# Placing the attention steps of batches 2 to 5 anew, with V moved on hardware queues and loads tied to slots

## The chip, the cores and the metric

The kernel runs on one core of a Trainium2 chip. The metric is the device time of one execution in microseconds (us), lower is better. Eight executions of the kernel before gave a median of 354.93 us, from 352.25 to 355.64. The profile shows one of these executions (352.25 us) in full; its span from the first to the last instruction is 350.5 us.

The engines are TensorE (PE in the profile; PEld is its weight load), VectorE (DVE), ScalarE (ACT), GpSimd (POOL) and SyncE (SP). DMAs are issued by POOL (a software queue, q0), or by SP and ACT (hardware queues, q1). Every engine runs its own instructions in the order of the program and waits on semaphores of the others.

## What is computed

Two stages, in float32 at the outside:

```python
batch, n_heads, seq, head_dim = (8, 8, 576, 64)
n_tokens, d_model, d_ff = (4608, 512, 2048)

def _attn_ref(q, k, v):                      # window = 64, causal
    scores = scale * np.matmul(q, k.transpose(0, 1, 3, 2))
    mask = (rel >= 0) & (rel < window)       # rel = query position - key position
    attn = softmax(np.where(mask, scores, -1e9))
    return np.matmul(attn, v)

def _moe_ref(x, w_in, w_out):
    h = x @ w_in
    return (h - np.tanh(h)) @ w_out
```

The attention's output, heads side by side, is x with 4608 rows of 512. The kernel computes in bf16 with float32 sums.

## The kernel before

**Units.** A batch b is one of 8 sequences of 576 tokens with 8 heads. A group g = 4b + pr is a pair of heads of a batch, 32 groups in all. A window j is 64 queries, 9 to a batch, each with 128 keys. A chunk c is 512 tokens of x, 9 in all; chunk 2 needs x of batches 1 and 2, chunk 3 of batches 2 and 3, chunk 4 of 3 and 4, chunk 5 of 4 and 5.

**The two-layer part.** `hp_mm(c, m)` is four matmuls of 512 columns for one of 16 slices m of the hidden layer (L393), then `Tanh` on ACT (L398); `g_sub(c, m)` subtracts on DVE and leaves gT (L405). `yp_mm` is four of the matmuls of the output (L417); every fourth one is followed by `y_out`, a copy on ACT (L422) and a DMA to the output on SP (L424). A hidden slice has a bank of PSUM: m % 3 in chunks 0 to 2, m % 2 after; the bank is free when `g_sub` has read it.

**Slots.** The order of all this is written out by hand as numbered slots. `OPS` gives each slot at most one piece of the two-layer part: slots 0 to 31 the hidden layer of chunk 0 (every second one), 32 to 47 the output of chunk 0, 48 to 63 hidden 1, 64 to 79 output 1, 80 to 95 hidden 2, and from 96 on hidden c and output c - 1 in turn, 32 slots to a chunk. `at(h, fn, ...)` hangs a step of the attention on slot h. The loop at the end of the kernel goes through the slots and emits, for each, first the two-layer piece, then its steps in the order of their `at` calls, then `g_sub`:

```python
for fn, args in items.pop(h, []):
    fn(*args)
if op and op[0] == "h":
    g_sub(*op[1:])
```

A slot is a place in the order and not a time: an engine that has nothing to wait for runs ahead of the others' slots.

**The steps of a group** from batch 2 on are: `cast` of q and of k (rows reordered into qb and kb, on DVE or POOL, L86), `tr` of q and of k (six transposes each on PE, L267, in bank 3; the q result goes out half on ACT and half on DVE, L84 and L86, the k result on ACT), `scores` three times (three matmuls each, L334, in bank 4, then `Exp` on ACT, L336), `masking` (DVE, L340), and the product with V. That product is `tile_pv` in batches 0 to 3 (20 matmuls of 65 columns, L322, banks 6 and 7, then one reciprocal and one multiplication on DVE, L326 and L328) and `pv` three times with `norm` in batches 4 to 7 (nine matmuls of 130 columns, L346, banks 5 to 7, then one reciprocal and two multiplications of 64 partitions, L353 and L357). The result xs is turned by `x_tr` (transposes on PE, L363, copied out on DVE or ACT) in batches 0 to 3 and by `x_dma` (two DMA transposes on SP, L378) in batches 4 to 7.

**V.** `load_v_all` brings V of a batch from DRAM (one buffer, vall), `cast_v` reorders it, four calls to a batch, into vb (one buffer as well), and nine `keys_v` or `windows_v` are DMAs from vb into vw, one per window (L161, L176; two buffers of vw, by the batch's parity). `pv` of windows 3i to 3i + 2 waits for these three.

**Loads** of q and k are issued on POOL, either per group (`load`, 144 KB as written) or per batch (`load_all`, 576 KB). `pace(h)` is a copy of one element on POOL that waits for the last `g_sub` before slot h, so that a load behind it doesn't start earlier.

Around the change the order before is this. Batch 0's nine `keys_v` and batch 1's are all on POOL. In slots 48 and 49 POOL has `cast_v(2)` four times, nine `windows_v(2)`, `load_v_all(3)`, and in slot 50 the eight loads of groups 12 to 15; in slots 55 and 56 it has the casts of group 10. Batch 3 is placed at slots 62 to 95, batch 4 from 69 on, batch 5 from 86 on.

## Time and profile before

| what | value |
|---|---|
| median of 8 executions (lowest, highest) | 354.93 us (352.25, 355.64) |
| profiled execution: its time, its span | 352.25 us, 350.5 us |
| granted TensorE clock, mean | 0.969 |
| PE, PEld busy | 318.8 us (91%), 173.3 us (49%) |
| DVE, ACT, POOL busy | 201.1, 184.9, 113.5 us (57, 53, 32%) |
| chain that ended last: PE, DMA, POOL, DVE, ACT | 67, 14, 7, 4, 3% of the span |
| start of slot 32, 48, 64, 80 | 41.44, 67.64, 92.69, 115.80 us |
| start of slot 96, 128, 160 | 143.03, 180.27, 214.07 us |

How to read it. The start of a slot is the start of its first L393 or L417 matmul in the timeline. Matmuls of 512 columns follow each other every 0.216 us, so four of them take 0.86 us in the chain of waits, although the page lists a mean of 385 ns for one; PE that counts as busy may still be waiting between two of them. A line of the timeline has the start, the time from the first start to the last end of a run of like instructions, the engine, the line of the kernel, the tiles and, in brackets, the idle time before it and what ended that.

### The profile page before, as it was taken

The page shows a single profiled execution, that of the slowest core. Times are in us where ns is not written, and L with a number is a line of the kernel's source. Part 1 is how long each engine was busy: PE and PEld are TensorE (multiplying, and loading weights), DVE is VectorE, ACT ScalarE, POOL GpSimd, SP SyncE. Part 2 cuts the span into 40 slices and gives each one's busy share as a digit, 9 for nine tenths or more (in the row PEclk, how much of TensorE's full clock was granted, in tenths as well). Part 3 has the DMA queues.
Part 4 walks back from the last instruction along what each step waited for, and adds up shares of the span by engine and source line. Part 5 has one row for each costly group of instructions (what it writes and reads, how often), then busy time and mean ns, then how long its engine had stood idle before and what let it go on. Part 6 is the DMA issues. An engine that isn't in the chain of part 4 may idle for free.

```text
span 350.5 us, 6289 instructions
## 1 busy us (share of the span) xinstructions
PE 318.8 (91%) x2452; PEld 173.3 (49%) x2452; DVE 201.1 (57%) x336; ACT 184.9 (53%) x336; POOL 113.5 (32%) x169
## 2 busy tenths in 40 slices
PE   6769989794999868899899999999999999999994
PEld 2544444452555544555555555555555444444442
DVE  4565766883665667577666767766666444444300
ACT  3534534584555767466566666655554444444411
POOL 8860166684713613362362553610000000000000
PEclk9568999999899999999999999999999999999999
DMA  8999999989399169528499598689921400100021
GB/s 156 149 178 215 194 166 154 174 138 165 45 154 236 51 98 163 76 61 139 100 160 166 107 170 145 126 163 211 191 63 51 109 30 30 55 36 30 32 90 61
DMA packets 51398, 42.39 MB, mean 121 GB/s; under 512 B 21176, under 2 KB 44664, under 8 KB 51368
## 3 DMA queue, kind: packets, MB, share of 16 engines
q0 software_dynamic: 21728, 20.40, 38.8%
q1 hardware_dynamic: 29432, 21.30, 26.0%
q8 instruction: 19, 0.31, 0.4%
q10 hardware_dynamic: 208, 0.29, 0.3%
q14 instruction: 11, 0.09, 0.1%
HBM read 36.70 MB, written 11.21 MB: 137 GB/s over the span
## 4 chain that ended last, share of the span: by engine, by line
PE 67%; DMA 14%; POOL 7%; DVE 4%; ACT 3%; issue 3%; POOLq 0%; ACTq 0%; DVEq 0%; SPq 0%
PE ps L417 30%; PE ps L393 27%; DMA vall<-in_v_dram 10%; PE ps L334 3%; PE ps L267 3%; PE ps L346 2%; POOL vw L176 2%; DMA qall<-in_q_dram 2%; DMA kall<-in_k_dram 1%; PE ps L322 1%; POOL vb L86 1%; POOL vw L161 1%; DVE gT L405 1%; DMA kt<-kd 1%; ACT pt L336 1%
## 5 line engine op out<-in xcount | busy, mean ns | idle before, releaser
L393 PE MATMUL ps<-xT,wi 128*128 128x512 bf16 x576 | 146.7, 385 | 3.1 <-DVE gT L405 2.4
L405 DVE TENSOR_TENSOR gT<-ps,th 128x512 bf16<-128x512 f32 x144 | 98.8, 690 | 84.1 <-ACT th L398 82.3
L417 PE MATMUL ps<-w_out_sb,gT 128*128 128x512 bf16 x576 | 143.9, 379 | 0.0
L398 ACT ACTIVATE th<-ps 128x512 f32<-128x512 f32 x144 | 85.6, 597 | 76.4 <-PE ps L393 74.9
L393 PEld LDWEIGHTS <-wi 128*128 128x128 bf16 x576 | 61.9, 114 | 52.0 <-issue 6.9
L417 PEld LDWEIGHTS <-gT 128*128 128x128 bf16 x576 | 53.3, 98 | 53.8 <-issue 0.2
L336 ACT ACTIVATE pt<-ps 128x384 bf16<-128x384 f32 x72 | 35.2, 489 | 31.7 <-PE ps L334 31.4
L86 POOL COPY vb<-vall 72x1024 bf16<-72x1024 bf16 x24 | 24.8, 1052 | 32.4 <-DMA vall<-in_v_dram 20.1
L422 ACT ACTIVATE ysb<-ps 128x512 f32<-128x512 f32 x36 | 21.6, 599 | 18.6 <-PE ps L417 18.6
L86 DVE COPY qt<-ps 64x576 bf16<-64x576 bf16 x20 | 15.2, 760 | 21.6 <-ACT qt L84 21.6
L334 PE MATMUL ps<-qt,kt 128*128 128x128 bf16 x216 | 23.9, 220 | 2.1 <-ACT pt L336 1.4
L357 DVE TENSOR_TENSOR xs<-ps,rc 64x576 bf16<-64x576 f32 x32 | 24.2, 755 | 0.8
L334 PEld LDWEIGHTS <-kt 128*128 128x128 bf16 x216 | 16.1, 98 | 12.3 <-issue 2.2
L340 DVE TENSOR_TENSOR pt<-pt,ps 128x1152 bf16<-128x1152 bf16 x24 | 17.9, 744 | 1.1 <-ACT pt L336 1.1
L346 PEld LDWEIGHTS <-pt 128*128 128x128 bf16 x144 | 12.0, 98 | 12.5 <-issue 1.3
L346 PE MATMUL ps<-vw,pt 128*128 128x130 bf16 x144 | 16.0, 220 | 1.0 <-DVE xs L357 1.0
L86 POOL COPY qb<-qall 96x768 bf16<-96x768 bf16 x15 | 12.4, 825 | 11.5 <-DMA qall<-in_q_dram 7.7
L86 POOL COPY kb<-kall 96x768 bf16<-96x768 bf16 x19 | 15.7, 832 | 0.0
L84 ACT ACTIVATE qt<-ps 64x576 bf16<-64x576 bf16 x20 | 12.7, 635 | 5.6 <-PE ps L267 5.6
L97 POOL DMA_DIRECT2D qall<-in_q_dram x15 | 9.7, 647 | 18.1 <-DMA vall<-in_v_dram 10.5
L267 PE MATMUL ps<-ident,qb 96*128 96x96 bf16 x120 | 8.6, 209 | 6.0 <-POOL qb L86 4.9
L84 ACT ACTIVATE kt<-ps 128x576 bf16<-128x576 bf16 x20 | 13.0, 648 | 1.4 <-PE ps L267 1.4
(74 smaller groups left out, 212.1 us busy)
## 6 DMA issues: line engine op xcount, KB each, us to landing
out_dram<-ysb SPq DMA_DIRECT2D x36, 256.0 KB, 2.1
vw<-vb SPq DMA_DIRECT2D x40, 130.0 KB, 4.2
vall<-in_v_dram POOLq DMA_DIRECT2D x7, 576.0 KB, 11.2
kall<-in_k_dram POOLq DMA_DIRECT2D x4, 576.0 KB, 9.5
qall<-in_q_dram POOLq DMA_DIRECT2D x4, 576.0 KB, 9.0
kall<-in_k_dram POOLq DMA_DIRECT2D x15, 144.0 KB, 10.2
qall<-in_q_dram POOLq DMA_DIRECT2D x15, 144.0 KB, 9.9
wi<-in_moe_w_in_dram POOLq DMA_DIRECT2D x2, 1024.0 KB, 11.3
```

What stands on the lines that cost most here:

```text
L84: nc.scalar.activation(o, i, ACT.Copy)
L86: eng.tensor_copy(o, i)
L267: nc.tensor.transpose(tp[:, e, :], src[:, e, :], ident[:P, :P])
L334: nc.tensor.matmul(sp[:, i, :], kT[g % NR][:, 64 * j:64 * j + 128], qT[g % NR][:, :, 64 * j:64 * j + 64], start=True, stop=True)
L336: nc.scalar.activation(PT[g % NPT][:, 3 * grp:3 * grp + 3, :], sp, ACT.Exp, scale=scale)
L346: nc.tensor.matmul(ps[:, 5 + grp, 130 * i:130 * i + 130], PT[g % NPT][:, j, :], vw[b % 2][:, j, 2 * pr:2 * pr + 2, :], start=True, stop=True)
L357: nc.vector.tensor_tensor(xo[r, :, :, pr, :], ov[r, :, :, h, 0:D], rc[r].to_broadcast([64, 3, 3, 64]), ALU.mult)
L393: nc.tensor.matmul(hp, w_in_tile(ki, m), chunk_tile(c)[:, :, ki % 2, 64 * (ki // 2):64 * (ki // 2) + 64], start=(ki == 0), stop=(ki == 3))
L398: nc.scalar.activation(th, hp, ACT.Tanh)
L405: nc.vector.tensor_tensor(gT[c][:, m, :], hp, th, ALU.subtract)
L417: nc.tensor.matmul(yp, gT[c][:, m, s * 128:(s + 1) * 128], w_out_sb[:, m, :], start=(m == 0), stop=(m == M - 1))
L422: nc.scalar.activation(ysb, ps[:, yp_bank(c, s), :], ACT.Copy)
```

## The change

Four things are done; the computation is the same.

1. `keys_v` of batch 0: windows 0 and 3 on SP, 1 and 4 on ACT, the other five on POOL. `keys_v` of batch 1: by turns on POOL and SP.
2. Batch 2: `cast_v` moves from POOL in slot 48 to DVE in slot 46; `windows_v` from POOL in slot 49 to SP in slot 47. Batch 3's loads become three loads of a whole batch at slots 54 (k, behind a `pace`), 55 (q) and 56 (v), in place of v at 49 and eight loads at 50. Its `cast_v` moves from slots 62 to 65 to 67 to 70, its `windows_v` from 67 to 71.
3. Groups 8 to 15 take their slots from a table, with `pv` and `norm` (all in one slot, `whole_pv`) in place of `tile_pv`. `x_tr` of batch 2 goes to bank 0, and batch 3 uses `x_dma` in slot 92 in place of four `x_tr`.
4. Batches 4 and 5 get other slots for groups, `cast_v`, `windows_v` and loads (batch 4's loads at 77, 78, 79 in place of 71, 72, 69; batch 5's at 97, 98, 99 in place of 86, 89, 92), the loads of batch 5 wait for `x_dma(3)` as well (`behind_x`), and `load_all` of batch 6 goes from slots 124 and 128 to 128 and 130. From slot 148 on the placing is as before.

```diff
--- before.py
+++ after.py
@@ -481,8 +481,8 @@
     copy_mask()
     tile_scores(0, 0, (0, 1))
     tile_scores(0, 1, (4, 5))
-    for j in range(NJ):
-        keys_v(0, j, G)
+    for j, eng in enumerate((Y, A, G, Y, A, G, G, G, G)):
+        keys_v(0, j, eng)
     load_w_in(0)
     load_w_in(1)
     load_w_out(0)
@@ -524,7 +524,7 @@
 
     at(33, lambda: [cast_v(1, pr, V) for pr in range(NP)])
     at(34, more_constants)
-    at(35, lambda: [keys_v(1, j, G) for j in range(NJ)])
+    at(35, lambda: [keys_v(1, j, (G, Y)[j % 2]) for j in range(NJ)])
     at(35, load, 7, "q", G)
     at(35, load_v_all, 2)
     for g in 8, 9, 10, 11:
@@ -561,68 +561,77 @@
     at(47, x_tr, 1, 1, 0, 4, 3, V)
     at(47, x_tr, 1, 1, 4, 9, 6, A)
 
+    at(46, lambda: [cast_v(2, pr, V) for pr in range(NP)])
+    at(47, lambda: [windows_v(2, j, Y) for j in range(NJ)])
+    at(54, pace, 54)
+    at(54, load_all, 3, "k")
+    at(55, load_all, 3, "q")
+    at(56, load_v_all, 3)
     for pr in range(NP):
-        at(48, cast_v, 2, pr, G)
-    at(49, lambda: [windows_v(2, j, G) for j in range(NJ)])
-    at(49, load_v_all, 3)
-    for g in range(12, 16):
-        at(50, load, g, "k", G)
-        at(50, load, g, "q", G)
+        at(67 + pr, cast_v, 3, pr, G)
+    at(71, lambda: [windows_v(3, j, Y) for j in range(NJ)])
     for i in range(2):
         at(140 + 4 * i, more_zeros, i)
 
-    def std(g, ck, cq, t, tk, ss, ms, p):
-        at(cq, cast, g, "q", V if g not in (10, 11, 15) else G)
-        at(ck, cast, g, "k", V if g not in (10, 11, 15) else G)
-        at(t, tr, g, "q", 3, A, V)
+    def whole_pv(g):
+        for i in range(3):
+            pv(g, i)
+        norm(g)
+
+    STEPS = {
+        8: (48, V, 50, 52, (55, 57, 59), 61, 63),
+        9: (52, V, 55, 57, (60, 61, 62), 64, 66),
+        10: (55, G, 60, 62, (64, 65, 66), 68, 70),
+        11: (59, G, 64, 65, (68, 69, 70), 71, 74),
+        12: (64, V, 67, 68, (72, 73, 74), 76, 78),
+        13: (68, V, 71, 72, (76, 77, 78), 80, 83),
+        14: (71, G, 75, 76, (80, 82, 84), 86, 88),
+        15: (75, G, 79, 81, (85, 86, 87), 88, 91),
+    }
+    for g, (c, eng, tq, tk, ss, ms, p) in STEPS.items():
+        at(c, cast, g, "q", eng)
+        at(c + 1, cast, g, "k", eng)
+        at(tq, tr, g, "q", 3, A, V)
         at(tk, tr, g, "k", 3, A)
         for i in range(3):
-            at(ss + 2 * i, scores, g, i, 4)
+            at(ss[i], scores, g, i, 4)
         at(ms, masking, g)
-        at(p, tile_pv, g, (6, 7))
-
-    for i, g in enumerate(range(8, 12)):
-        a = (50, 55, 60, 65)[i]
-        lead = 3 if i < 2 else 5
-        std(g, a - lead + 1, a - lead, a, a + 2, a + 3, a + 8, a + (12 if i == 0 else 11))
-    at(70, x_tr, 2, 0, 0, 4, 3, V)
-    at(71, x_tr, 2, 0, 4, 9, 3, A)
-    at(78, x_tr, 2, 1, 0, 4, 3, V)
-    at(79, x_tr, 2, 1, 4, 9, 3, A)
-
-    for g in range(3 * NP, B * NP):
+        at(p, whole_pv, g)
+    at(71, x_tr, 2, 0, 0, 4, 0, V)
+    at(72, x_tr, 2, 0, 4, 9, 0, A)
+    at(77, x_tr, 2, 1, 0, 4, 0, V)
+    at(78, x_tr, 2, 1, 4, 9, 0, A)
+    at(92, x_dma, 3)
+
+    def behind_x(b):
+
+        last = ((b + 1) * NJ - 1)
+        nc.gpsimd.tensor_copy(tick, chunk_tile(last // WPC)[0:1, last % WPC, 0, 0:1])
+
+    LOADS = {4: (77, 78, 79), 5: (97, 98, 99), 6: (128, 130, 113)}
+    for g in range(4 * NP, B * NP):
         b, pr = divmod(g, NP)
-        a = 8 * g - 48 - (0, 2, 4)[min(b - 3, 2)]
-        s = 32 * b - (0, 2, 4)[min(b - 3, 2)]
+        a = 8 * g - 52
+        s = 32 * b - 4
         cv, ky = s - 72 + 5 * pr, s - 54
-        if b == 3:
-            a = (68, 73, 78, 82)[pr]
-            cv = 62 + pr
-        elif b == 4:
-            a = 84 + 7 * pr
-            cv, ky = 75 + 3 * pr, 86
+        if b == 4:
+            a = (89, 95, 101, 108)[pr]
+            cv, ky = 91 + pr, 95
         elif b == 5:
-            cv, ky = 95 + 4 * pr, 108
+            a = 110 + 7 * pr
+            cv, ky = 108 + pr, 112
+        elif b == 6:
+            cv = 118 + 4 * pr
         at(cv, cast_v, b, pr)
-        if b == 3:
-            lead = 3 if pr < 3 else 6
-            std(g, a - lead + 1, a - lead, a, a + 2, a + 3, a + 8, a + 11)
-            if pr == 0:
-                for j in range(NJ):
-                    at(67, windows_v, b, j, Y)
-            if pr % 2:
-                at(a + 12, x_tr, b, pr // 2, 0, 4, 3, V)
-                at(a + 13, x_tr, b, pr // 2, 4, 9, 3, A)
-            continue
         if b < 7:
-            at(a - 7, cast, g, "q")
+            at(a - (5 if b < 6 else 7), cast, g, "q")
             at(a, tr, g, "q", 3, A, V)
         else:
             at(a - 14, cast_q, g)
             at(a - 12, bounce, g, "q")
             at(a - 6, tr_dma, g, "q")
         if b < 7:
-            at(a - 5, cast, g, "k")
+            at(a - (4 if b < 6 else 5), cast, g, "k")
             at(a + 2, tr, g, "k", 3, A)
         else:
             at(a - 13, cast, g, "k")
@@ -638,16 +647,14 @@
             at(a + 16, x_dma, b)
         for j in range(NJ):
             if pr == 0:
-                at(ky + (j // 2 if b > 5 else 0), windows_v, b, j, Y)
+                at(ky + j // 2, windows_v, b, j, Y)
         if pr == 0:
-            if b > 3:
-                hq, hk = s - (60 if b < 7 else 68), s - (64 if b < 7 else 72)
-                hv = {4: 69, 5: 92}.get(b, s - 78)
-                if b < 6:
-                    hk, hq = {4: (71, 72), 5: (86, 89)}[b]
-                for h, f in (hv, (load_v_all, b)), (hq, (load_all, b, "q")), (hk, (load_all, b, "k")):
-                    at(h, pace, h)
-                    at(h, *f)
+            hk, hq, hv = LOADS.get(b, (s - 72, s - 68, s - 78))
+            for h, f in (hv, (load_v_all, b)), (hq, (load_all, b, "q")), (hk, (load_all, b, "k")):
+                at(h, pace, h)
+                if b == 5:
+                    at(h, behind_x, 3)
+                at(h, *f)
 
     for h in range(32 * NC + 32):
         op = OPS.get(h)
```

## The prediction

> **What bounds the kernel now.** I read the busy times by stage first, cut at the starts of slots 32, 48, 64, 80, 96 and 128. Columns: stretch, its length, busy time and (instructions) of PE, PEld, DVE, ACT, POOL, then clock, DMA share, GB/s.
>
> ```profile
> 41.44:67.64 26.20, 22.04 (x284) 12.00 (x283) 18.27 (x39) 11.53 (x20) 15.38 (x23) 1.00 1.09 178
> 67.64:92.69 25.05, 19.39 (x144) 10.67 (x142) 16.04 (x26) 15.19 (x30) 18.32 (x28) 0.93 0.79 122
> 92.69:115.80 23.11, 21.28 (x237) 12.04 (x234) 12.76 (x24) 12.08 (x26) 6.27 (x10) 1.00 0.87 160
> 115.80:143.03 27.23, 21.42 (x221) 12.64 (x216) 20.04 (x33) 20.05 (x40) 10.70 (x15) 1.00 0.65 104
> 143.03:180.27 37.24, 36.09 (x278) 20.87 (x278) 25.40 (x40) 22.91 (x44) 16.80 (x21) 1.00 0.57 99
> 180.27:350.50 170.23, 165.58 (x954) 86.33 (x952) 84.80 (x130) 82.94 (x146) 24.56 (x36) 1.00 0.47 100
> ```
>
> PE's own work I count from start-to-start distances in the timeline: 0.864 us for a two-layer piece (four at 0.216), 0.25 for a `tr`, 0.17 for `scores` or a third of `pv`, 0.54 for `tile_pv`, 0.055 for a transpose of x. That gives 20.84, 16.96, 20.30, 19.76 and 35.04 us for the first five stretches, so PE loses 5.36, 8.10, 2.81, 7.46 and 2.20 us in them, 25.9 in all, and only 0.9 in the last. The change lies in these five.
>
> The chain of waits from 60 to 100 us (start, length, what) shows the largest loss:
>
> ```profile
> 64.88 4.03 POOL vb L86 x4
> ...
> 74.16 11.23 DMA vall<-in_v_dram
> ...
> 86.29 0.85 POOL qb L86
> ...
> 87.19 0.66 PE ps L267 x6
> 87.85 2.83 PE ps L393 x8
> ```
>
> and the timeline says why:
>
> ```profile
> 80.32 0.63 POOL L97 DMA_DIRECT2D kall<-in_k_dram  x1
> ...
> 85.67 0.63 POOL L97 DMA_DIRECT2D qall<-in_q_dram  x1 [4.72 <-DMA vall<-in_v_dram]
> ...
> 87.19 0.66 PE L267 MATMUL ps<-ident,qb 96*128 96x96 bf16 x6 [4.85 <-POOL qb L86]
> ```
>
> POOL issues V of batch 3 and seven of eight loads, then stands still until V has landed; the cast of group 10 is queued behind, and PE waits 4.85 us. Each of POOL's stalls of this kind (four more from 25 to 42 us, one at 64.25) ends when the oldest of eight loads lands, so I read it as eight in flight at most. After the wait eight matmuls take 2.83 us in place of 1.73.
>
> Two other losses: slot 37's transposes wait for a cast that stands in DVE's queue behind V of batch 1 (landed 44.9), and hidden 2 loses 7.5 us in pieces of 0.5 to 1.3 to evacuations of bank 3 and to ACT and DVE, each 20 us busy of 27:
>
> ```profile
> 47.93 0.43 PE L287 MATMUL ps<-ident,kb 96*128 96x96 bf16 x6 [1.14 <-DVE kb L86]
> ...
> 128.97 0.41 PE L267 MATMUL ps<-ident,kb 96*128 96x96 bf16 x6 [1.06 <-ACT xT L84]
> ```
>
> [...] `windows_v` issued on SP lands in 3.8 us with no load near and in 7.2 to 9.4 beside one. [...] Here an issue of vall takes 0.85 us, its landing 7.4 to 13.5 beyond batch 1. [...] here `cast_v` is 1.05 us against 0.43.
>
> **The change, part by part**, in the profile's own time (350.5 span, 352.25 for that execution).
>
> *Start to slot 48.* POOL loses 4 of 9 `keys_v`, each about 0.58, and four places of the eight: the first w_in, issued at 16.08, goes at about 13, and all loads behind it land some 2.5 us earlier, V of batch 1 at 42.3. Two issues on ACT (0.4 to 0.7 each, between 11.15 and 12.5) push ACT's chain of batch 0 by 0.1 to 0.6; hidden 0 waits 0.49 for w_in now, so its start moves -0.5 to +0.6, I take -0.15. Slot 37's wait, 1.33 with its tail, goes: -1.5 so far. In batch 1 POOL issues 5 `keys_v` in place of 9, so V of batch 2 is issued at about 48.5 in place of 52.74 and lands (11.2 later at most) by 60, just before DVE wants it. But four `cast_v` on DVE, 4 x 0.43 = 1.72, now stand before batch 1's last products, where DVE has 0.2 to 0.4 us free and x of batch 1 is next: +1.5. With V late they would cost up to 2 us more. Hidden 1 starts at 67.6, as before.
>
> *Hidden 1.* POOL's 20.6 us (4 casts of V, 9 moves, 9 loads, 4 casts) shrink to 6.0, and three loads are far from eight: the cast of group 10 is done at about 79, its transposes come at 81. The wait and the cold clock go. Left are PE's work of 16.9 and DVE's sum of 17.6 (16 `g_sub` at 0.69, casts, two masks, one norm), which I price at 2 us of loss: 18.9 in place of 25.05. Slot 64 at 86.5, -6.2.
>
> *Output 1.* PE's work rises by 0.7 (batch 3's groups come earlier). The waits of bank 3 go, DVE's backlog (norm 0.21 + 2 x 0.755 = 1.72 in place of 1.04 for each of eight groups) costs about as much. Here V is the question. The load of k is tied to slot 54: issue 76.7; k, q, v together take some 15.5 (8 small loads and V took 14.1 from 77.2 to 91.3): V of batch 3 lands at 92.2. `cast_v` 4.2 to 96.4, nine moves on SP, 10 to 12 us to the last landing (11 in batch 5's case now): 108.5. Slot 78 has `pv(12)` and would come at 106 or 107. So slot 80 is at about 110.5, -5.3.
>
> *Hidden 2.* Two `tile_pv` and three x transposes fewer for PE (17.55 us of work), ACT falls from 20.5 to 15.6, DVE stays at 20.0 and leads: masks 13 to 15, norms 13 to 15, `g_sub` and one copy make 16.6 until norm 15, which ends 17.2 after slot 80, at 127.7. `x_dma(3)` lands 3.4 later (median of the first ones; 3.3 to 4.7 over all), where four x transposes, 1 us, and their evacuations stood. Slot 96 at about 131.4, -11.6.
>
> *Slots 96 to 127.* Loads of batch 5 wait for `x_dma(3)`: k issued at 134, V landed at 152, later than the 146.6 now. `cast_v` to 156.4, moves until 167 to 170, beside V of batch 6. On POOL `cast_v(6)` stands before the cast of group 22 and must wait until the moves have read vb; so `tr(22)` in slot 124 is ready at 170.4, against 165.9 for PE. `pv(20)` also stands directly behind `pv(19)` in slot 123 and waits for a norm, 1.9. In all 5.4 given back: slot 128 at 174.0 in place of 180.27, -6.2.
>
> *After.* `load_all(6)` is one to two slots nearer to its use; now q lands 1.5 us ahead of need. I take 0.6 (0 to 2). The rest, without loss now, stays.
>
> Sum: -1.5 + 1.5 - 6.2 + 0.9 - 6.3 + 5.4 + 0.6 = -5.6: 352.25 becomes 346.6. That execution was the fastest of eight, 2.7 below the median; on the median I predict 349.3.
>
> **Rivals.** A measurement of this kernel can tell 0.5% (1.8 us) from no change.
> 1. *The chain of V keeps up.* Loads and moves a few us faster than taken, and nothing is given back after slot 96: -11.6, 343.3. For it: moves with no load beside them land in 3.8. Against: V of batch 5 lands later than now by the sum above.
> 2. *V late from batch 3 on: slower.* From slot 78 on the path runs V landed, casts on POOL, moves on SP, norm, `x_dma(3)`, loads of batch 5, one us for one. If V of batch 3 lands at 97.8 in place of 92.2 all is gone; 1.8 later still it is slower. Batch 4's three loads now take 22.3 from first issue to last landing (94.72 to 117.02) beside nine moves; that puts V at 99, +1.2, and the same again in batch 5 about +3: 359. Against: no moves stand beside batch 3's loads in the new order.
> 3. *The stall stays under another name.* Group 10's casts are still on POOL, behind two or three large issues; if these block as the small ones did, the 4.85 us remain and with the extra DVE work the gain is near 0: 355. Against: batches 4 and 5 issue three such loads now without a stop over 1.04.
>
> **How the numbers follow.** Forecast 0.45, rival 1 0.23, rival 2 0.22, rival 3 0.10. The range reaches from rival 1 (342.5) to most of rival 2 (358); the forecast's own is 346 to 352.5. Faster by over 0.5%: the forecast but a few per cent, and rival 1, 0.64; within: 0.12; slower: 0.24.
>
> **What would show it.** No wait of `tr` for qb near slot 60 and hidden 1 near 19 us (rival 3 if not); slot 37 without a wait; four vb copies on DVE of 0.43 each without a wait before them; last moves of batch 3 landed at 108 to 109, and a wait of `pv(12)` of 1 to 3 us; slot 96 at 131 (over 136: rival 2); a wait of slot 124's transposes for qb of 3 to 5 us (none: rival 1). If hidden 1 saves less than 4 us, or DVE waits for V in slot 46, the forecast is wrong from there.

## The result, and the profile after

The changed kernel takes 359.25 us (median of 11 executions, 355.89 to 362.15), the kernel before 354.28 in the same session (32 executions). The ratio is 1.0129, with a 95% interval from 1.0100 to 1.0158: slower by 1.3%, where 349.3 us was predicted. The profiled execution took 359.56 us, its span 357.8 us. Here and below the ratios leave out executions more than 1.5% above the fastest of their kernel (9 of 22 of `a_win4`, 2 of 6 of `c_three`) and the medians don't, so a ratio can differ by up to 0.4% from what two medians give.

Each kernel has a second profile (`before_look` and `after_look`, single executions of 351.92 and 357.38 us, below), so there are two values. "Predicted" is in the profile's own time. "After against predicted" takes the first profile.

| start of | before | predicted | after | after against predicted |
|---|---|---|---|---|
| slot 48, hidden 1 | 67.64 / 71.26 | 67.6 | 67.81 / 67.77 | +0.2 |
| slot 64, output 1 | 92.69 / 92.28 | 86.5 | 88.97 / 87.58 | +2.5 |
| slot 80, hidden 2 | 115.80 / 115.37 | 110.5 | 116.04 / 114.51 | +5.5 |
| slot 96 | 143.03 / 142.59 | 131.4 | 139.71 / 138.17 | +8.3 |
| slot 128 | 180.27 / 179.83 | 174.0 | 186.97 / 184.92 | +13.0 |
| end of span | 350.5 / 350.2 | 344.9 | 357.8 / 355.7 | +12.9 |

The change leads by 3.7 us at slot 64, and by 3.3 at slot 96; between 96 and 128 it loses 10.0. The prediction misses 2.3, 3.0, 2.8 and 4.7 us in four stages in a row. The busy times by stage of the changed kernel, cut at the starts of slots 32, 48, 64, 80, 96 and 128 (stretch, length, busy time and instructions of PE, PEld, DVE, ACT, POOL, clock, DMA share, GB/s):

```profile
41.90:67.81 25.91, 22.36 (x283) 12.51 (x282) 18.97 (x43) 11.53 (x20) 9.78 (x16) 0.96 1.06 183
67.81:88.97 21.16, 20.39 (x129) 10.88 (x128) 13.43 (x24) 15.35 (x30) 5.67 (x8) 0.88 0.74 112
88.97:116.04 27.07, 21.98 (x211) 13.81 (x209) 20.44 (x31) 13.81 (x28) 10.33 (x15) 1.00 0.72 134
116.04:139.71 23.67, 18.52 (x141) 10.97 (x138) 20.20 (x32) 15.31 (x29) 8.58 (x10) 1.00 0.28 55
139.71:186.97 47.26, 40.34 (x291) 22.84 (x291) 24.84 (x39) 24.06 (x47) 19.22 (x28) 0.93 0.72 125
186.97:357.80 170.83, 166.14 (x954) 86.33 (x952) 86.22 (x132) 82.84 (x146) 25.50 (x37) 1.00 0.46 101
```

Counted as in the prediction (starts' distances less PE's own work), PE loses 5.1, 4.4, 6.1, 6.2 and 11.6 us in the first five. The last stretch is 0.6 longer than before, as predicted. In output 1 DVE is busy for 20.4 us of 27.1, where it was 12.8 of 23.1.

The timeline of the changed kernel around slot 48 (start, length, what, idle time before it and what ended it):

```profile
60.80 0.63 POOL L97 DMA_DIRECT2D qall<-in_q_dram  x1 [5.08 <-DMA vall<-in_v_dram]
61.71 1.42 DVE L86 COPY vb<-vall 72x1024 bf16<-72x1024 bf16 x4
...
66.88 1.14 PE L363 MATMUL ps<-ident,xs 128*128 128x128 bf16 x9 [1.59 <-DVE xs L328]
...
67.81 5.17 PE L393 MATMUL ps<-xT,wi 128*128 128x512 bf16 x12
```

V of batch 2 is there in time and DVE copies it without a wait, but the last x of batch 1 is late for PE by 1.59 us (1.24 before), and then the twelve matmuls of slot 48 take 5.17 us, 0.43 each and not 0.22 (granted clock 0.50 from 67.81 to 72.70). At slot 60 there is no wait for group 10's cast any more (0.21 us lost).

The same timeline in output 1, slots 64 and 65:

```profile
89.57 1.52 DVE L357 TENSOR_TENSOR xs<-ps,rc 64x576 bf16<-64x576 f32 x2
90.00 0.42 PE L267 MATMUL ps<-ident,qb 96*128 96x96 bf16 x6
92.25 4.16 POOL L86 COPY vb<-vall 72x1024 bf16<-72x1024 bf16 x4 [8.30 <-DMA vall<-in_v_dram]
92.49 0.76 DVE L86 COPY qt<-ps 64x576 bf16<-64x576 bf16 x1
93.28 2.20 DVE L86 COPY qb<-qall 96x768 bf16<-96x768 bf16 x1
93.30 0.41 PE L267 MATMUL ps<-ident,kb 96*128 96x96 bf16 x6 [1.85 <-DVE qt L86]
95.40 1.21 DVE L86 COPY kb<-kall 96x768 bf16<-96x768 bf16 x1
```

K's transposes want bank 3 one slot after Q's; DVE's half of Q's copy stands behind a normalisation of 1.52 us, a `g_sub` and a mask multiplication, so PE waits 1.85. The next two casts take 2.20 and 1.21 us in place of 0.35, beside POOL's copies of V, and make slot 68 wait in its turn. V of batch 3 itself landed at 92.2, to the tenth where it was predicted, but by luck: the load of k was issued at 78.45 and not at 76.7, and the three loads took 13.7 us and not 15.5. In the second profile V landed at 90.65.

From slot 95 on (only the lines of the wait):

```profile
134.18 2.93 SPq L378 DMA_TRANSPOSE xT<-xs  x2
...
137.21 0.65 SPq L176 DMA_DIRECT2D vw<-vb  x1
137.95 7.84 SPq L161 DMA_DIRECT2D vw<-vb  x8
138.17 0.76 DVE L86 COPY qt<-ps 64x576 bf16<-64x576 bf16 x1 [0.86 <-ACT qt L84]
138.97 0.69 DVE L405 TENSOR_TENSOR gT<-ps,th 128x512 bf16<-128x512 f32 x1
139.71 1.02 PE L393 MATMUL ps<-xT,wi 128*128 128x512 bf16 x4 [2.47 <-DVE gT L405]
...
152.33 0.22 PE L346 MATMUL ps<-vw,pt 128*128 128x130 bf16 x1 [1.17 <-DMA vw<-vb]
153.76 0.22 PE L346 MATMUL ps<-vw,pt 128*128 128x130 bf16 x1 [1.22 <-DMA vw<-vb]
```

The nine windows of batch 4 stand on SP behind the x transfer of batch 3, which waits for the normalisation of group 15; POOL's copies of V of batch 4 had been done since 124.6. In slot 104 PE waits for the windows, and slots 105 to 107 run slowly after it (slot 106's four matmuls in 1.91 us and not 1.03, granted clock 0.50 from 154.62 to 158.03): 4.4 us lost. The chain of waits (start, length, what) has the same places among its longest pieces:

```profile
68.02 4.98 PE ps L393 x12
...
93.28 2.20 DVE qb L86
95.48 1.13 DVE kb L86
...
144.95 8.77 DMA vw<-vb
```

Five more slots, 110, 115, 117, 120 and 123, lose 1.21, 0.74, 0.76, 0.65 and 2.03 us. In 110, 115 and 117 a step of group 20 stands in the slot of a step of group 19 that uses the same bank, and in 123 directly behind its normalisation; in 120 PE waits for ACT's copy of an output.

### The profile page after: what moved, and what is told of

The parts are those of the page before. It is cut to its first block, busy times and chain, and to the rows that moved or that the text cites. A ratio compares the mean times of both kernels' runs of the same rounds, so it can differ in the third digit from the quotient of the medians.

```text
span 357.8 us, 6075 instructions
## 1 busy us (share of the span) xinstructions
PE 322.6 (90%) x2346; PEld 176.5 (49%) x2346; DVE 208.0 (58%) x344; ACT 183.1 (51%) x332; POOL 98.6 (28%) x148
## 4 chain that ended last, share of the span: by engine, by line
PE 66%; DVE 15%; DMA 9%; ACT 5%; issue 2%; SPq 2%; POOL 1%; ACTq 0%; DVEq 0%; POOLq 0%
PE ps L393 29%; PE ps L417 28%; DMA vw<-vb 4%; DVE xs L357 3%; DVE gT L405 3%; PE ps L346 3%; DVE qt L86 3%; PE ps L334 2%; PE ps L267 2%; DMA vall<-in_v_dram 2%; DMA kt<-kd 2%; ACT qt L84 1%; SPq L161 1%; DVE xs L328 1%; ACT th L398 1%
## 5 line engine op out<-in xcount | busy, mean ns | idle before, releaser
L393 PE MATMUL ps<-xT,wi 128*128 128x512 bf16 x576 | 149.4, 390 | 6.4 <-DVE gT L405 6.2
L417 PE MATMUL ps<-w_out_sb,gT 128*128 128x512 bf16 x576 | 145.9, 382 | 0.5 <-ACT ysb L422 0.5
L357 DVE TENSOR_TENSOR xs<-ps,rc 64x576 bf16<-64x576 f32 x48 | 36.2, 755 | 1.2
L422 ACT ACTIVATE ysb<-ps 128x512 f32<-128x512 f32 x36 | 21.4, 595 | 19.1 <-PE ps L417 18.9
L86 POOL COPY vb<-vall 72x1024 bf16<-72x1024 bf16 x20 | 20.8, 1061 | 28.2 <-DMA vall<-in_v_dram 16.9
L334 PE MATMUL ps<-qt,kt 128*128 128x128 bf16 x216 | 24.0, 221 | 1.9 <-ACT pt L336 1.2
L346 PE MATMUL ps<-vw,pt 128*128 128x130 bf16 x216 | 21.7, 220 | 4.3 <-DMA vw<-vb 2.4
L346 PEld LDWEIGHTS <-pt 128*128 128x128 bf16 x216 | 16.8, 98 | 15.9 <-issue 3.3
L334 PEld LDWEIGHTS <-kt 128*128 128x128 bf16 x216 | 17.0, 99 | 14.8 <-issue 5.1
L86 POOL COPY qb<-qall 96x768 bf16<-96x768 bf16 x16 | 13.3, 834 | 26.1 <-DMA qall<-in_q_dram 26.1
L267 PE MATMUL ps<-ident,kb 96*128 96x96 bf16 x120 | 8.6, 209 | 5.4 <-DVE qt L86 5.3
L452 POOL COPY tick<-gT 1x1 bf16<-1x1 bf16 x13 | 2.5, 189 | 39.6 <-DVE gT L405 39.6
## 6 DMA issues: line engine op xcount, KB each, us to landing
vall<-in_v_dram POOLq DMA_DIRECT2D x7, 576.0 KB, 11.6
```

The source lines that it names most:

```text
L86: eng.tensor_copy(o, i)
L334: nc.tensor.matmul(sp[:, i, :], kT[g % NR][:, 64 * j:64 * j + 128], qT[g % NR][:, :, 64 * j:64 * j + 64], start=True, stop=True)
L346: nc.tensor.matmul(ps[:, 5 + grp, 130 * i:130 * i + 130], PT[g % NPT][:, j, :], vw[b % 2][:, j, 2 * pr:2 * pr + 2, :], start=True, stop=True)
L357: nc.vector.tensor_tensor(xo[r, :, :, pr, :], ov[r, :, :, h, 0:D], rc[r].to_broadcast([64, 3, 3, 64]), ALU.mult)
L393: nc.tensor.matmul(hp, w_in_tile(ki, m), chunk_tile(c)[:, :, ki % 2, 64 * (ki // 2):64 * (ki // 2) + 64], start=(ki == 0), stop=(ki == 3))
L417: nc.tensor.matmul(yp, gT[c][:, m, s * 128:(s + 1) * 128], w_out_sb[:, m, :], start=(m == 0), stop=(m == M - 1))
```

## The experiments

Each ratio is to the kernel before on the chip of that run. A stage's length differs by up to 3 us from one execution to the next even ahead of an edit (slots 32 to 47: 25.7 to 28.8 us in the changed kernel's variants), so the stage of the edit and the ratio are read together.

| kernel | median, us | ratio | 95% interval |
|---|---|---|---|
| the change | 359.25 | 1.0129 | 1.0100 to 1.0158 |
| a_win4 | 354.83 | 1.0000 | 0.9974 to 1.0026 |
| a_apart | 359.29 | 1.0169 | 1.0124 to 1.0215 |
| c_win4_apart | 354.44 | 0.9996 | 0.9967 to 1.0025 |
| a_tile_pv | 358.15 | 1.0108 | 1.0061 to 1.0154 |
| a_cast_pool | 361.05 | 1.0229 | 1.0195 to 1.0264 |
| c_three | 349.77 | 0.9862 | 0.9817 to 0.9908 |
| c_tk | 352.01 | 0.9931 | 0.9895 to 0.9967 |
| c_six | 352.62 | 0.9964 | 0.9936 to 0.9993 |
| a_v2_pool | 357.59 | 1.0128 | 1.0084 to 1.0171 |
| a_v2_48 | 357.45 | 1.0114 | 1.0078 to 1.0150 |
| a_v2_held | 358.52 | 1.0133 | 1.0076 to 1.0191 |
| b_load3 | 352.84 | 0.9946 | 0.9910 to 0.9983 |
| b_keys | 350.57 | 0.9892 | 0.9866 to 0.9918 |
| b_keys_again | 350.66 | 0.9894 | 0.9844 to 0.9944 |
| b_keys_load3 | 349.56 | 0.9863 | 0.9826 to 0.9900 |

### The windows of batch 4 and the neighbours in one slot

`a_win4`:

```diff
-            cv, ky = 91 + pr, 95
+            cv, ky = 86 + pr, 90
...
-                at(ky + j // 2, windows_v, b, j, Y)
+                at(ky + (j // 2 if b > 4 else 0), windows_v, b, j, Y)
```

> The changed kernel with V of batch 4 cast in slots 86 to 89 and all its windows issued in slot 90, ahead of the x transfer of batch 3 in SP's order. Theory 3 (the windows stand on SP behind that transfer, which waits for the normalisation of group 15, and then run beside the loads of batch 5): slot 104 waits for no window (2.4 us in the changed kernel), slots 105 to 107 keep their full rate (1.7 us), and the time falls by 3 to 4.5 us. If the windows cover for another lateness there: the 2.4 us come up in slots 105 to 117 under another name, and the time is within 1 us. V of batch 4 has to have landed by slot 86 for it.

The ratio falls from 1.0129 to 1.0000, 4.6 us (3.6 by the medians). The casts move too, but they had been done at 124.6 in the changed kernel as well. In the timeline the windows are issued at 125 and the x transfer after them; slot 104's products wait for nothing:

```profile
125.29 0.64 SPq L176 DMA_DIRECT2D vw<-vb  x1
126.03 7.49 SPq L161 DMA_DIRECT2D vw<-vb  x8
...
135.34 2.89 SPq L378 DMA_TRANSPOSE xT<-xs  x2
149.47 0.33 PE L346 MATMUL ps<-vw,pt 128*128 128x130 bf16 x3
150.68 0.33 PE L346 MATMUL ps<-vw,pt 128*128 128x130 bf16 x3
151.97 0.33 PE L346 MATMUL ps<-vw,pt 128*128 128x130 bf16 x3
```

Slots 104 to 107 lose 0.2 us and not 4.4, slots 96 to 127 take 42.9 us and not 47.3, and the x transfer isn't later for it (at slot 95's start less 1.8 us in both). `c_win4_apart` and `c_three`, with the same order on SP, lose 0.2 us in slot 104 too. So this one place in SP's order is the largest cost of the change that a single edit took away.

`a_apart`:

```diff
-            a = 110 + 7 * pr
+            a = 111 + 7 * pr
```

> The changed kernel with all steps of batch 5's groups one slot later (start 111 + 7 pr in place of 110 + 7 pr). Theory 4 (in slots 110, 115, 117, 120 and 123 steps of groups 19 and 20 stand in one slot and share a bank or follow directly on each other's normalisation, 1.21 + 0.74 + 0.76 + 0.65 + 2.03 us lost): three to five of these losses go, stage 96 to 127 falls from 47.3 to 42.5 to 44.5 us, and the time falls by 2.5 to 4.5 us. If the losses come from DVE and ACT being busy and not from who stands in one slot: they move to the neighbouring slots and the time is within 1 us of the changed kernel (358 to 360).

> The changed kernel with two edits together: windows of batch 4 ahead of the x transfer (as a_win4) and batch 5 one slot later (as a_apart). a_apart alone gave nothing, though slots 110 to 127 lost 2.3 us less, since its slot 104 waited 1.7 us more for the windows of batch 4. Theory 4 (the slots' neighbours cost 2 to 2.5 us once nothing else waits for DMA there): stage 96 to 127 falls from 42.9 us (a_win4) to about 40.5, and the ratio from 1.000 to 0.993 to 0.995. Rival (what batch 5 gains by one slot is lost in its last slots or after 127): ratio 0.998 to 1.003.

The losses in slots 110, 115, 117 and 123 go; 0.2 to 1.1 stay or come up in 111, 112, 120, 121, 124 and 127, so slots 110 to 127 lose some 2.3 us less. In `a_apart` slot 104's wait grows from 2.4 to 3.9 us instead, and there is no gain. With the windows ahead (`c_win4_apart`) slots 96 to 127 take 40.9 us, but the ratio, 0.9996, can't be told from `a_win4`'s: the 2 us are seen in the stage of one profile and not in the times. The expectation of 0.993 to 0.995 is missed.

### DVE's work in output 1 and hidden 2

`a_tile_pv` and `a_cast_pool`:

```diff
-        at(p, whole_pv, g)
+        at(p, tile_pv, g, (6, 7))
```

```diff
-        12: (64, V, 67, 68, (72, 73, 74), 76, 78),
-        13: (68, V, 71, 72, (76, 77, 78), 80, 83),
+        12: (61, G, 67, 68, (72, 73, 74), 76, 78),
+        13: (63, G, 71, 72, (76, 77, 78), 80, 83),
```

> The changed kernel with the P times V of groups 8 to 15 done as before (one piece with two rows of banks, and no separate normalisation of 1.5 to 1.7 us on DVE for all three). Theory 1 (DVE's work and its order set output 1 and hidden 2): DVE loses some 0.7 us of work for each of eight groups, so 20.4 us busy in output 1 fall to about 17.5, PE loses 2 to 4 us less from slot 64 to slot 96, and the time falls by 2 to 4 us. Theory 4 (the stages from slot 64 on are held by steps that share a bank or stand in one slot) and the rival that transfers hold it: within 1 us of the changed kernel, 358 to 360.

> The changed kernel with the casts of groups 12 and 13 on POOL in slots 61 to 64, where POOL stands idle from 83.9 to 92.2 us, in place of DVE in slots 64 to 69, where two of them took 2.20 and 1.21 us beside POOL's cast of V. Theory 1a (these two, slowed by POOL at the same time, make DVE late for the copies that empty bank 3): slots 65 and 68 lose under 0.5 us in place of some 3 together, output 1 falls from 27.1 to 24 us, and the time falls by 2 to 3. If DVE's backlog comes from the normalisations alone: output 1 over 26 us, the time within 1 us of the changed kernel. If POOL is late for it: group 11's cast comes later and slot 64 waits instead.

The waits of K's transposes in slots 65 and 68 were 1.85 and 1.74 us. `a_cast_pool`'s timeline has

```profile
94.50 0.41 PE L267 MATMUL ps<-ident,kb 96*128 96x96 bf16 x6 [1.86 <-DVE qt L86]
99.17 0.42 PE L267 MATMUL ps<-ident,kb 96*128 96x96 bf16 x6 [0.56 <-DVE qt L86]
```

and `a_tile_pv`'s

```profile
91.68 0.42 PE L267 MATMUL ps<-ident,kb 96*128 96x96 bf16 x6 [1.01 <-DVE qt L86]
96.38 0.42 PE L267 MATMUL ps<-ident,kb 96*128 96x96 bf16 x6 [0.56 <-DVE qt L86]
```

So slot 65's extra 0.85 us is the longer normalisation, slot 68's extra 1.2 the casts that take 2.20 and 1.21 us beside POOL's copies, and 0.55 stays in both: one slot is too short for the two copies. The 1.2 isn't there in every execution: in `c_win4_apart` the same cast takes 0.84 us and not 2.20, and slot 68 waits 0.56. Theory 1 is right about the waits and wrong about the time. With `a_tile_pv` hidden 2 falls from 23.7 to 21.5 us and slot 96 begins at 136.0 in place of 139.7, but the ratio is 1.0108: slots 104 and 105 now lose 4.9 us for the windows. With `a_cast_pool` slot 78 waits 1.85 us for windows of batch 3, and the ratio gets worse; its profile, 1.5 us longer in span than that of the change, doesn't show all of that 1%.

`c_three` has the edits of `a_win4`, `a_apart` and `a_tile_pv` together:

> The changed kernel with three edits: windows of batch 4 ahead of the x transfer, batch 5 one slot later, and P times V of groups 8 to 15 in one piece as before (as a_tile_pv). a_tile_pv alone began slot 96 3.7 us sooner than the changed kernel and gave it back in slot 104, waiting for windows. Theory (each of the three is a cost of its own, and the windows only hid the other two): 1.2 to 2.2 per cent below the changed kernel by the windows and batch 5, and another 0.7 to 1 by P times V, a ratio of 0.984 to 0.990. If DVE's work from slot 64 to 95 is hidden anyway: as c_win4_apart, within 0.3 per cent.

The ratio is 0.9862, in the expected range, 2.6% below the change, and 1.3% below `c_win4_apart`, from which only P times V differs, though `a_tile_pv` alone gave 0.2%. What DVE costs counts once SP's order no longer hides it. Its busy times by stage, slots 48, 64, 80 and 96 on (columns as above):

```profile
66.67:86.52 19.85, 18.88 (x141) 10.46 (x139) 13.45 (x24) 15.15 (x30) 5.69 (x8) 0.95 0.78 118
86.52:112.66 26.14, 22.51 (x258) 13.22 (x253) 16.44 (x26) 13.80 (x28) 10.30 (x14) 1.00 0.73 134
112.66:135.17 22.51, 18.50 (x173) 10.23 (x171) 17.66 (x28) 15.33 (x29) 8.71 (x10) 1.00 0.66 108
135.17:175.07 39.90, 37.13 (x291) 21.56 (x291) 24.66 (x39) 23.41 (x46) 17.64 (x26) 1.00 0.69 125
```

DVE's 20.4 and 20.2 us have become 16.4 and 17.7, and slots 96 to 127 take 39.9 us. Output 1 is still 26.1. SP's order now costs something the other way round: the normalisation of group 15 ends at 128.73, but SP is issuing the windows of batch 4 until 130.19 and comes to the x transfer of batch 3 at 130.30, and slot 95 loses 3.48 us waiting for that transfer, where the changed kernel lost 2.47 to DVE. `c_tk` is `c_three` and gives K's transposes of groups 11 to 14 two slots after Q's again (`11: (59, G, 64, 66, ...` and so on), and `c_six` is `c_tk`, holds V of batch 2 as `a_v2_held` below, and calls batch 3's loads for slots 51 to 53:

> c_three with the transposes of K of groups 11 to 14 two slots after those of Q, as the kernel before has them, in place of one. Theory (one slot of 1.0 us is too short for the two copies that empty bank 3, so slots 65, 68, 72 and 76 lose 1.19, 0.73, 0.71 and 0.73 us in c_three): these 3.4 us go. Then either PE comes to slot 78 so much sooner and waits there for V's windows of batch 3 (1.5 us in c_three), which takes all of it back, so the ratio stays at 0.985 to 0.988; or half of it remains, 0.981 to 0.984. I take the first.

> c_tk with V of batch 2 held as in a_v2_held and batch 3's three loads called for in slots 51 to 53 in place of 54 to 56, so that V lands some 3 us sooner. If the three remaining losses (slot 48's half rate 1.4 us, bank 3 in output 1 3.4 us, V's windows in slot 78) are all real and the earlier V lets them go: 4 to 5 us below c_three, a ratio of 0.972 to 0.976. If POOL's order (cast of V of batch 2, then the loads, then the casts of groups 10 and 11) is late instead: a wait in slot 60 or 64 for a cast, and a ratio no better than c_three's 0.986.

In `c_tk` the waits of 65, 68 and 76 are gone (72 waits 1.11 for a copy of x), and slot 78, which PE reaches at 107.4 in place of 108.2, loses 3.0 us to windows of batch 3 and slot 79 another 1.1 to slow matmuls (ahead of it, three of L334 took 0.50 us and not 0.33): 26.9 us for the stage, ratio 0.9931. In `c_six` output 1 takes 24.6 us, but slots 55, 63 and 69 lose 1.7, 1.9 and 1.6, and 95 to 98 lose 6.5. Both miss what was expected of them: `c_six` is slower than `c_three`, and `c_tk` isn't faster (their intervals overlap slightly).

### V of batch 2 ahead of slot 48

`a_v2_pool` has `G` for `V` in slot 46, `a_v2_48` is on POOL in slot 48 as before, and `a_v2_held` waits there for the last x:

```diff
-    at(46, lambda: [cast_v(2, pr, V) for pr in range(NP)])
-    at(47, lambda: [windows_v(2, j, Y) for j in range(NJ)])
+    at(48, lambda: behind_x(1))
+    at(48, lambda: [cast_v(2, pr, G) for pr in range(NP)])
+    at(49, lambda: [windows_v(2, j, Y) for j in range(NJ)])
```

> The changed kernel with the cast of V of batch 2 on POOL in slot 46 in place of DVE. Theory 2 (the four casts on DVE delay x ahead of slot 48, PE stands 1.59 us and then runs twelve matmuls at half their rate): the wait ahead of slot 48 goes, the twelve matmuls take 2.6 us and not 5.2, hidden 1 falls from 21.2 to about 19 us, and the time falls by 2 to 3.5. If the half rate has another cause: slot 48 stays at 5 us and the time within 1 us. A cost that may show instead: POOL is busy for 4 us and windows of batch 2 come 2 us later, or group 10's cast.

> The changed kernel with the cast of V of batch 2 on POOL in slot 48, where the kernel before has it, its windows on SP in slot 49. The run with the cast on POOL in slot 46 kept the wait ahead of slot 48 (1.62 us) and the half rate (twelve matmuls 5.28 us), and there DVE's two multiplications by the mask took 1.66 us and not 0.82 while POOL copied. Theory 2b (any copy of V that runs in slots 46 and 47, on DVE or beside it, makes the last x late, and PE's wait leaves it slow): the wait ahead of slot 48 falls under 0.5 us, the twelve matmuls take 3 to 4 us, slot 48 begins 1 us sooner, and the time falls by 2 to 3.5 us. Rival (the tail of the first attention waits for its own chain on ACT and DVE, and the half rate is PE's lasting state there): within 1 us of the changed kernel.

> The changed kernel with V of batch 2 cast on POOL and held there until the last x of batch 1 is copied (end of slot 47), so that neither DVE nor POOL copies V in slots 46 and 47. Unheld on POOL (a_v2_48) the copy ran from 62.2 us, DVE's two mask multiplications took 2.32 us in place of 0.91 in the kernel before, and PE stood 1.62 us ahead of slot 48 and not 1.24. Theory 2c (V's copy, on either engine, makes x late by 0.4 us, and PE falls to half rate after the longer wait): the wait falls to 1.24, slot 48 from 5.3 to 3.3 us, hidden 1 from 21.2 to about 18.9 us, and the time by 2 to 2.5 us against the changed kernel, a ratio of 1.005 to 1.008 to before. Rival (the rate has another cause): slot 48 stays at 4.2 us or more, a ratio of 1.011 to 1.015.

Unheld, POOL copies V as soon as it has landed, whatever its slot (from 62.24 us in `a_v2_48`), and PE waits 1.62 us in both kernels. Held, the timeline has

```profile
63.20 0.90 DVE L313 TENSOR_TENSOR pt<-pt,mask_sb 128x640 bf16<-128x640 bf16 x2
...
66.50 0.68 PE L363 MATMUL ps<-ident,xs 128*128 128x128 bf16 x9 [1.24 <-DVE xs L328]
66.57 4.16 POOL L86 COPY vb<-vall 72x1024 bf16<-72x1024 bf16 x4 [0.50 <-DMA out_dram<-ysb]
67.02 2.75 PE L393 MATMUL ps<-xT,wi 128*128 128x512 bf16 x12
...
87.76 0.22 PE L346 MATMUL ps<-vw,pt 128*128 128x130 bf16 x1 [0.86 <-DMA vw<-vb]
```

The wait and the rate are as expected (wait 1.24, the twelve matmuls in 2.75, slot 48 in 3.30 us), the time isn't: the windows now come late for slot 63, which loses 1.5, slot 51 loses 0.4, and the ratio is 1.0133. What is late next is the next product with V, here as in `c_tk` and, below, `b_load3`.

### The parts alone, on the kernel before

`b_load3` takes batch 3's loads and the windows of batch 2 on SP from the change, `b_keys` the three queues for V of batches 0 and 1, `b_keys_load3` both:

```diff
-    for j in range(NJ):
-        keys_v(0, j, G)
+    for j, eng in enumerate((Y, A, G, Y, A, G, G, G, G)):
+        keys_v(0, j, eng)
...
-    at(35, lambda: [keys_v(1, j, G) for j in range(NJ)])
+    at(35, lambda: [keys_v(1, j, (G, Y)[j % 2]) for j in range(NJ)])
```

> The kernel before with only the loads of batch 3 as the change has them (three loads of a whole batch, held to slots 54 to 56, K first and V last) and the windows of batch 2 on SP; every step keeps its old slot. The step of the prediction that priced this (the wait for group 10's cast, 4.85 us, and the slow matmuls after it go): hidden 1 falls from 25.1 to about 19 us and the time by 4 to 6 us against before, so 348 to 350, if nothing is late next. Rival (the loads come late for the old slots: K, Q and V of batch 3 land 3 to 7 us later than they did): output 1 grows by as much, and the time is within 1 us of before.

> The kernel before with only the moves of V to the key layout of batches 0 and 1 spread over three queues, as the change has them. The prediction priced this, with slot 37's wait of 1.33 us, at about -1.5: V of batch 1 lands 1 to 1.5 us sooner, slot 37 loses nothing, and the time falls by 1 to 1.5 us, a ratio of 0.996 to 0.997. Rival (the wait only moves to the tail of the stage, in slots 46 and 47, where ACT and DVE end last): ratio 0.999 to 1.002. In the changed kernel h0 began 1.07 us later than before (two issues on ACT took 1.20 and 1.22 us); if that is theirs, it shows here too.

> The kernel before with two parts of the change: V's moves over three queues, and batch 3's loads as three whole-batch loads in slots 54 to 56; the steps stay in their old slots. If the two gains add (0.989 and 0.995): ratio 0.982 to 0.985, 348 us. If both remove the same wait (group 10's cast in slot 60) and V of batch 3 is late for the old slot 78, as in b_load3 (6.5 us lost there): ratio 0.989 to 0.996, no better than the moves alone. What is then left between this kernel and the changed one, some 2 per cent, belongs to the new slots and to the loads of batches 4 and 5.

`b_load3`: hidden 1 takes 18.9 us, the number that the prediction gave, and group 10's wait is gone. Output 1 then takes 28.7 in place of 23.1, because PE comes to slot 79, where group 12's product with V stands, at 105.8 and not at 113.3 and meets the windows of batch 3; some lines of the timeline:

```profile
109.11 0.22 PE L322 MATMUL ps<-vw,pt 128*64 128x65 bf16 x2 [0.97 <-DMA vw<-vb]
...
110.49 0.22 PE L322 MATMUL ps<-vw,pt 128*64 128x65 bf16 x2 [0.66 <-DMA vw<-vb]
111.38 0.27 PE L322 MATMUL ps<-vw,pt 128*64 128x65 bf16 x2 [0.67 <-DMA vw<-vb]
```

Of 6.2 us saved 0.5% remains. `b_keys` alone is worth 1.1%, more than priced; both together 1.4%, which lies between the two forecasts, and the interval doesn't tell whether the gains add. The kernel with both is 2.6% below the change, so the rest of the change (the casts of V of batches 2 and 3 in other places, the new slots of batches 2 to 5, P times V with `norm`, the loads of batches 4 and 5) costs 2.6% when it is added, as much as the three edits of `c_three` take away again.

Since the profile of `b_keys` was of an execution above its median, there are further profiles of it and of both kernels:

> The same kernel as b_keys (before with only the moves of V to the key layout spread over three queues), looked at once more, since its profiled execution began hidden 1's work 2.8 us late and showed little of its gain. If the gain is real: ratio 0.986 to 0.992, and in a profile that begins near 25.4 us group 10's wait in slot 60 (4.85 us before) is down by 3 us or more, which is the wait that the prediction put to the loads of batch 3 alone. If the gain was chance: ratio 0.995 to 1.0.

> The kernel before, unchanged, looked at a second time, since its only profile is that of its fastest execution (352.25, where its median is 354). If an ordinary execution loses more in slot 37 or slot 60 than the profile shown (1.33 and 4.85 us): these waits are 1 to 3 us longer here, and that is what b_keys takes away. If not: as in the profile shown within 0.5 us, and b_keys' gain lies elsewhere.

> The kernel of b_keys looked at a third time; its two profiles are of executions 2.4 and 2.6 us above its median. If it is the wait for group 10's cast that it shortens: slot 60 waits 2 us or less here, and the execution is at 350 or below. If it is the start: hidden 0 and slot 32 begin 1 to 2 us sooner than in the kernel before.

> The changed kernel, unchanged, looked at a second time, to see which losses of its stages come back in every execution. Theory: the losses that follow from the order of the steps (slots 65, 68, 72, 76 in output 1, 90, 93 and 95 in hidden 2, 110, 115, 117 and 123) are there again within 0.1 us each, 5.9, 5.2 and 4.7 us in all; the one that follows from transfers (slot 104) differs by 1 us or more.

The gain came again (0.9894). The profiles don't locate it: `b_keys` waits 3.82 and 4.21 us at slot 60 in two of three (0.39 in the other, which began hidden 1 late), and its slot 128 begins at 179.2 and 179.4 there, 0.4 to 1.1 sooner than in the two of before. Both profiled executions of the kernel before (352.25 and 351.92) are some 2 us below its medians, so what an ordinary one loses hasn't been seen.

`before_look` shows something else. The kernel before, with no wait at slot 60:

```profile
63.59 4.03 POOL L86 COPY vb<-vall 72x1024 bf16<-72x1024 bf16 x4
64.93 3.37 DVE L313 TENSOR_TENSOR pt<-pt,mask_sb 128x640 bf16<-128x640 bf16 x2
...
68.01 0.69 PE L322 MATMUL ps<-vw,pt 128*64 128x65 bf16 x20 [1.47 <-DVE pt L313]
...
70.33 1.14 PE L363 MATMUL ps<-ident,xs 128*128 128x128 bf16 x9 [1.62 <-DVE xs L328]
71.26 5.18 PE L393 MATMUL ps<-xT,wi 128*128 128x512 bf16 x12
```

POOL's copies of V of batch 2 began 1.3 us sooner and met DVE's mask multiplications, which cost PE 2.5 us in slots 46 and 47; slots 37 to 39 lost another 2.5. Slot 48 began 3.6 us later, and group 10's cast was then in time. Slot 64 begins at 92.28 against 92.69: the losses on both sides share one slack.

In the second profile of the change the losses that I put to the order of steps are there again: slots 65, 68, 72 lose 2.0, 1.8 and 1.3, slots 90, 93, 95 lose 1.43, 1.16 and 2.65, and 110, 115, 117, 120 and 123 the same to 0.01. So is that of slot 76, 0.7. Slots 104 to 107 lose 4.1 where I expected a difference of 1 us or more from the first profile's 4.4.

## Why the prediction was wrong

In short, four steps failed, one in each stage from slot 48 to slot 127. The prediction let PE keep its full rate in slot 48, and the half rate (granted clock 0.50) cost 2.0 us in that slot (`a_v2_held` takes them away, and then the next product with V is late). In output 1 it put the DVE work that comes at about the waits of bank 3 that go, and the stage took 3.0 more. In hidden 2 it let slot 96's piece start with x, and a bank held that piece (the stage took 2.8 more). From slot 96 on it left out SP's order, in which nine windows stand behind an x transfer (4.4); what it did expect there, V of batch 5 late in slot 124, did not come.

*Start to slot 48: right in its sum, in part by luck.* Slot 37's wait is gone in both profiles, V of batch 2 landed at 60.5 ("by 60"), DVE copied it without a wait, and slot 48 began at 67.8 for 67.6. But slot 32 began 0.46 us later than before and not earlier, and DVE's copies cost 1.0 us in slots 46 and 47 and not 1.5, so two errors cancelled. Two terms were empty: w_in was issued at 12.85 us as said, but landed at 25.34 against 25.32, so an earlier place in the queue brought its data no sooner; and the two issues on ACT took 1.20 and 1.22 us, not 0.4 to 0.7.

*Hidden 1: the wait went, the price was wrong, by 2.3 (0.9 in the second profile).* "The wait and the cold clock go" was half true: the wait for group 10's cast and the slow matmuls behind it went (granted clock 0.50 from 87.85 to 89.96 us before), and slow matmuls came in slot 48. The stage saved 3.9 us, less than the 4 that the prediction had named as the sign of being wrong from there. The 1.5 us for DVE's copies ahead of slot 48 were in the sum, but not that PE was at half rate after the longer wait there (1.59 in place of 1.24, granted clock 0.50 and not 1.00); slot 48 lost 2.4 us where it had lost 0.5. Beyond that, the 6.2 us were taken from one execution; in `before_look` the same place costs nothing and slot 64 isn't sooner. Up to slot 64 the change got 3.7 us between the first profiles and 4.7 between the second. More could be had: `b_load3` begins slot 64 at 85.20, 7.5 us sooner than before.

*Output 1: the first step whose mechanism failed, by 3.0.* "The waits of bank 3 go, DVE's backlog costs about as much": priced +0.9 with the stage at 24.0, measured 27.1 and 26.9. I had counted the normalisation's extra work, but not where it stands: ahead of the copy that frees bank 3, with K's transposes moved to one slot after Q's. The parts measured are 0.55 us in each of four slots from the short distance, 0.85 from the normalisation in slot 65, 1.2 from casts on DVE beside POOL's copies in slot 68 (2.20 us for one of 0.35). V of batch 3 was at the right place by luck (92.2; the 15.5 us for its loads rested on 14.1 counted from 77.2, though V had been issued at 74.16 there), and `pv(12)` had no wait only because PE came later, at 113.1; where PE came at 108.2 (`c_three`), slot 78 lost 1.5 us.

*Hidden 2: mis-sized by 2.8.* The last normalisation ended 18.1 us after slot 80 (17.2 predicted) and the x transfer wasn't what held slot 96: the prediction let slot 96's piece start when x was there, but that piece uses the bank of slot 95's, and waits 2.47 us for a `g_sub` that DVE does behind the copy of group 17's Q. The x transfer is what holds slot 96 only in `c_three` and the two kernels built on it.

*Slots 96 to 127: the right sign, another cause, 10.0 in place of 5.4.* I named V of batch 5 and a wait in slot 124. There was none. Only the wait of `pv(20)` behind group 19's normalisation in slot 123 was named rightly (1.9 predicted, 2.03). The rest has three parts. The windows of batch 4 behind the x transfer on SP cost 4.4 (shown by `a_win4`, 4.6 in the time). Group 20 beside group 19 costs 3.4 besides slot 123; of the 5.4 together `a_apart` takes 2.3 away in the stage, and nothing that can be told in the time. Slots 97 and 98 at half rate after slot 95's wait (granted clock 0.50 from 140.97 to 144.38) cost 1.7. I had followed V through POOL and the transfers but not each DMA's place in SP's order.

*After slot 128:* +0.6, as predicted. That the later `load_all` of batch 6 is the cause isn't shown: in the three profiles of `b_keys`, one kernel, this stretch differs by up to 2.6 us.

*The rivals.* The second gave 359 us, and that this is nearly the time is luck: it had V of batch 3 late, at 99, and V was there at 92.2. The third's stall on POOL did not come. The first is excluded.

*What stays open:* where `b_keys`' 1.1% lies; why `a_cast_pool` is 1% slower than the change (0.5% by the medians); whether moving batch 5 by a slot is worth anything by itself.

The fastest versions are two: before with V's moves on three queues and batch 3's loads whole (0.9863), and the change with three edits (0.9862).

## What to carry to other kernels

When a step is moved, go through every queue that it issues on and write down what stands ahead of it there: nine short moves behind one transfer that waits for DVE cost as much here (4.4 us) as the change had gained up to slot 64 (3.7 and 4.7). A wait in one profile is worth at most the distance to what is late next; look at a second execution before pricing it, and ask which transfer PE meets when it comes sooner. Two copies that empty one bank need a distance that holds with everything that stands ahead of them on their engine (a distance of one slot cost 0.55 us in each of four slots here), and repairs are judged together, since one wait can hide the gain of another.

## What had not been expected of the hardware

- Some of DVE's operations took much longer beside POOL's copies of V. A mask multiplication (L313) took 3.03 us in `before_look` and ended 0.3 us after POOL's fourth copy; the next, a little smaller, took 0.41. In the changed kernel a cast of 0.35 us (qb<-qall) took 2.20. Others kept their time there: the copy qt<-ps took 0.76 us beside POOL's copies, as elsewhere, and the multiplication xs<-ps,rc 0.82 in `b_keys_again`. Why some took longer and others didn't isn't shown.
- PE's half rate didn't go with the length of the wait alone. After a wait of 1.59 or 1.62 us the twelve matmuls of slot 48 took 5.17 us in the changed kernel, 3.62 in `after_look`, 3.64 in `c_three`, 4.91 in `a_v2_48`, 5.28 in `a_v2_pool`, 5.18 in `before_look`, and 2.75 in `b_keys_third`. After a wait of 1.24 us they took 2.75 in the kernel before and in `a_v2_held`, but 3.89 in `a_win4`, where waits of 1.36 and 1.17 us stood ahead of them. The granted clock over these matmuls, first in the changed kernel, then in the kernel before (columns as above):

```profile
67.81:72.70 4.89, 4.89 (x14) 1.81 (x13) 1.00 (x3) 1.74 (x4) 0.00 (x0) 0.50 0.90 138
67.64:70.23 2.59, 2.59 (x16) 1.34 (x14) 1.78 (x4) 1.43 (x4) 2.29 (x4) 1.00 0.30 47
```

  What sets the clock after such a wait isn't shown.
- A move of V issued on SP took 0.54 to 1.86 us of SP in the changed kernel (median 0.76 for L161, 0.65 for L176), and the two on ACT took 1.20 and 1.22 us of ACT; the prediction had 0.4 to 0.7 for each of these two.
